# A fourth Strassen pair in four blocks of a fused attention and GEGLU kernel, with its helper sums and snapshots moved between engines

## The chip, the cores and the metric

The kernel runs on one core of a Trainium2 chip. The time is the device time of one execution in microseconds; for the kernel before it is the median of 8 runs. A profile records one execution instruction by instruction. Its engines are PE (TensorE, matrix multiply, with its weight loads listed apart as PEld), DVE (VectorE), ACT (ScalarE), POOL (GpSimd) and SP (SyncE, which issues DMAs here). Each engine works through its own instruction queue in order and waits on semaphores for the others.

## The reference

The computation is a linear attention followed by a gated feed-forward block. Inputs are q, k, v of 8 batches x 8 heads x 576 positions x 64, and three weight matrices of a width of 512 and a hidden width of 1536.

```python
q_s = np.exp(q - q.max(-1, keepdims=True)); q_s /= q_s.sum(-1, keepdims=True)
k_s = np.exp(k - k.max(2, keepdims=True));  k_s /= k_s.sum(2, keepdims=True)
kv = np.einsum('bhsd,bhse->bhde', k_s, v)
attn = np.einsum('bhsd,bhde->bhse', q_s, kv)
x = attn.transpose(0, 2, 1, 3).reshape(4608, 512)
g = x @ w_gate
out = (gelu(g) * (x @ w_val)) @ w_out
```

## The kernel before

**Blocks.** The 4608 rows are worked through in nine blocks: 0 to 7 hold 512 rows of each batch, and block 8 holds the 64 rows that each batch has over. The order is 0 to 6, then 8, then 7 (`order`, line 530). All matrices are in fp16 with sums in PSUM, which has eight banks; a small ring of bank names (`big`, `let_go`, lines 80 to 94) hands them out in turn.

**Hidden tiles.** For each block the hidden width is cut into 12 tiles of 128 (0 to 11). For each tile, g = x @ w_gate and v = x @ w_val are computed with the tile's rows as partitions, ScalarE takes Gelu of g and VectorE multiplies it with v into `ht`. Blocks 0 and 1 do this tile by tile (`ffn_fi`, line 475). From block 2 on a written-out list of steps sets the order of the work (lines 610 to 614): an entry such as `6g` or `6v` is one half of a tile done plainly (`half`, line 617: four matmuls of 512 columns), an entry such as `0.1` to `0.4` is one quarter of a pair (`pair_step`, line 627), and a single word such as `a`, `n` or `s0` is a place where other work rides along (`ride`, line 976, with the plan of lines 945 to 973).

**Pairs.** A pair k stands for the two tiles k and k + 3 and is computed as one 2 x 2 block product by Strassen's method in Winograd's form: seven products instead of eight, each of four matmuls of 256 columns (`product_gv`, line 594). Its quarters are: .1, products 1 and 5; .2, products 6 and 3; .3, products 7 and 2; .4, product 4. They run in three banks (pga, pgb, pgc). Between the products other engines work on the banks: ScalarE copies pga to pgb (line 660) and takes two snapshots `snq` (line 640; the one of product 5 is on VectorE in blocks 8 and 7, line 638), VectorE adds a snapshot to a bank into `cc` (line 644; the buffer alternates with one that lies in `eq`), and `final` finishes a lower quarter of a tile: Gelu on ScalarE (line 630), multiplication into `ht` on VectorE, here called the gate (line 631). `upper` finishes both upper quarters of the pair: Gelu in place on ScalarE (line 648), multiplication on GpSimd, or for pair 8 on VectorE (line 650). For pair 8 `upper` is put off until after the next entry of the list (lines 677 and 688).

A product writes to a bank only when the copy or add that reads it has finished: product 6 waits for the copy, product 7 for the second snapshot, product 3 for the first, product 4 for the add out of pga.

The list `THREE` (blocks 2 to 6) has the pairs 0, 1, 2 and the other six tiles in halves; `SIX` (blocks 8 and 7) has all six pairs 0, 1, 2, 6, 7, 8. Pairs need sums of weight blocks (`sum_wgv`, line 579) and of x (`sum_x`, line 588, on GpSimd). The weight sums for the pairs 6 to 8 are made on VectorE, three tiles at a time, one or two sums in each of the blocks 2 to 6 (line 972). Sum 3 writes over the weights that it reads.

**Output product.** `out_strassen` (line 722) multiplies `ht` by w_out in the same seven-product form with banks psa, psb, psc (`product`, line 702); the order is 1, 2, 5, 6, 3, 7, 4, and from block 2 on the tiles come in the order 0, 3, 1, 4, 2, 5 within a product. It needs sums of `ht` (`sum_h`, line 565): sums 1 and 2 on VectorE, 3 and 4 on GpSimd; the list has them at `s0`, `u0`, `s1`, `u1`, and the last two tiles' sums follow inside `out_strassen` (`last_js`). Snapshots `sn` (line 738) and adds into `yo` (line 748) are on VectorE, and the finished rows are stored by DMA.

**Riding work.** In each of the blocks 2 to 6 the attention of the next batches rides along. At `a` and `n`, `norm_pair` (line 235) sums exp(q) over the head width on VectorE and multiplies by the reciprocal on GpSimd; at `t`, `unit_td` transposes the result by a DMA; at `l`, the batch after next is loaded; at `e`, inside product 1 of the output, ScalarE takes the exponentials of q and k; at NS 0 the k-v product is made, and at NS 4 the next x (`unit_x4`, line 421), whose copies are split between ScalarE and VectorE. `cast_v` converts v on GpSimd at NS 2. `norm_rem0` and `unit_trem` do the same for the 64 rows that batch 0 has over.

Of the kernel before, what the change touches and what calls it, by code (L numbers as in the profile page):

```python
# [18 lines left out]
def kernel(  # L19
# [215 lines left out]
    def norm_pair(b, g, n0, engs):  # L235

        n = NC - n0
        e = buf(eq_b, b)[:, n0:NC, 2 * g * P:(2 * g + 2) * P].rearrange("p n (h d) -> p n h d", d=D)
        rq = att.tile([P, n, 4], f32, name="rq2", tag="rq2", bufs=2)
        nc.vector.reduce_sum(rq, e, axis=mybir.AxisListType.X)  # L240
        rrq = att.tile([P, n, 4], f32, name="rrq2", tag="rrq2", bufs=2)
        nc.vector.reciprocal(out=rrq, in_=rq)  # L242
        for j, eng in enumerate(engs):
            st[(b, "norm", 2 * g + j)] = (e[:, :, 2 * j:2 * j + 2], rrq[:, :, 2 * j:2 * j + 2], n)
            norm_mul(b, 2 * g + j, eng)
# [30 lines left out]
    st = {}  # L276
# [301 lines left out]

    def sum_wgv(nm, i, k=0, n=NO // 2):
        w = wg_sb if nm == "g" else wv_sb  # L580
        lo, hi = slice(k * P, (k + n) * P), slice((k + NO // 2) * P, (k + NO // 2 + n) * P)
        a11, a21, a12, a22 = w[:, 0:2, lo], w[:, 0:2, hi], w[:, 2:4, lo], w[:, 2:4, hi]
        t = [ws[(nm, k // NO)][:, j, :, k % NO * P:(k % NO + n) * P] for j in range(3)]
        o, a, b, op = {1: (t[0], a21, a22, ALU.add), 2: (t[1], t[0], a11, ALU.subtract),
                       3: (a21, a11, a21, ALU.subtract), 4: (t[2], a12, t[1], ALU.subtract)}[i]
        nc.vector.tensor_tensor(out=o, in0=a, in1=b, op=op)

# [6 lines left out]
    def product_gv(i, ps, xt, k, first):  # L594
# [3 lines left out]
        for t, w, nm in ((0, wv_sb, "v"), (1, wg_sb, "g")):  # L598
            ss = ws[(nm, k // NO)]
            for c in range(2):  # L600
# [8 lines left out]

    THREE = ("a 6g l 6v 0.1 9g 0.2 9v 0.3 7g 0.4 n 1.1 t 7v 1.2 10g 1.3 s0 10v 1.4 2.1 u0 8g 2.2 s1"  # L610
             " 8v 2.3 u1 11g 2.4 11v")
    SIX = ("0.1 6.1 0.2 6.2 0.3 6.3 0.4 1.1 6.4 7.1 s0 1.2 7.2 1.3 u0 7.3 1.4 2.1 7.4 8.1 s1 2.2"
           " 8.2 2.3 u1 8.3 2.4")
    steps = {b: (SIX if b >= B - 1 else THREE).split() for b in range(2, B + 1)}
    live = {}
# [11 lines left out]
    def pair_step(b, xt, k, i):  # L627
# [38 lines left out]
        if i == 2:  # L666
            product_gv(6, pa, xt, k, False)
            s2 = snap(pa)
            product_gv(3, pc, xt, k, False)
            add(cc[:, 0], pc, s2)  # L670
            let_go(pc)
        elif i == 3:
            product_gv(7, pa, xt, k, False)
            add(cc[:, 1], pa, s5)
            product_gv(2, pb, xt, k, False)
            final(pb, k)
            if k == NFI - NO // 2 - 1:
                live["upper"] = lambda: upper(cc)
            else:
                upper(cc)  # L680
        else:
            product_gv(4, pa, xt, k, False)
            final(pa, k + NO // 2)

    def go_on(b, xt, upto=None):
        while steps[b] and upto != 0:
            x = steps[b].pop(0)
            late = live.pop("upper", None)
            if "." in x:
# [32 lines left out]
    def out_strassen(b, last):  # L722
# [14 lines left out]

        def snap(nm):
            sn = ffn.tile([P, 2, 256], f32, name="sn", tag="gl")
            for n, (t, src) in enumerate(parts(nm)):  # L740
                if n:
                    nc.scalar.activation(out=sn[:, t], in_=src, func=ACTF.Copy, scale=1.0 / _H_SCALE)
                else:
                    nc.vector.tensor_scalar(out=sn[:, t], in0=src, scalar1=1.0 / _H_SCALE,
                                            scalar2=None, op0=ALU.mult)
            return sn
# [8 lines left out]
        get("a")  # L755
        product(1, ps["a"], True, js=js[:4])
        ride(b, NS, 0)
        if b >= B - 1:
            pair_step(b, get_x(b), NFI - NO // 2 - 1, 4)
        ride(b, PR, "e")  # L760
        get("b")
        product(1, ps["a"], False, js=js[4:])
        sum_h(*last_js(b), (1, 2))
        s1 = snap("a")
        product(2, ps["b"], True, js=js)
# [6 lines left out]
        sum_h(*last_js(b), (3,), "pool" if b > 1 else "dve")  # L772
        s5 = snap("c")
        ride(b, NS, 1)
        product(6, ps["a"], False, js=js)
        s2 = snap("a")
        ride(b, NS, 2)
# [167 lines left out]
    for b in range(2, B):  # L945
        n = b + 1
        if n < B:
            at(b, PR, "a", L(norm_pair, n, 0, 0, ("pool", "pool")))
            at(b, PR, "n", L(norm_pair, n, 1, 0, ("pool", "pool")))
            at(b, PR, "t", L(unit_td, n))  # L950
# [5 lines left out]
    at(4, PR, "e", exp_rem0)  # L956
    at(6, PR, "t", L(unit_trem, 0))
    for b in range(2, B - 1):
# [5 lines left out]
        at(b, NS, 4, L(lambda n: sum_x(get_x(n)), n if n < B - 1 else B))  # L964
        if b == 5:
            at(b, NS, 4, norm_rem0)
    at(B, NS, 2, L(lambda: sum_x(get_x(B - 1), xs_b[1])))
    for b in range(2, B + 1):
        for j in range(NO // 2 - 1):
            at(b, PR, f"s{j}", L(sum_h, j, NO, (1,)), L(sum_h, j, NO, (3,), "pool"))  # L970
            at(b, PR, f"u{j}", L(sum_h, j, NO, (2,)), L(sum_h, j, NO, (4,), "pool"))
    for b, x in ((2, "g1"), (2, "g2"), (3, "v1"), (3, "v2"), (4, "g4"), (5, "v4"), (6, "g3"), (6, "v3")):
        at(b, NS, 2, L(sum_wgv, x[0], int(x[1]), NO, NO // 2))

# [67 lines left out]
```

## Time and profile before

| | |
|---|---|
| median of 8 runs | 296.94 us (296.82 to 297.18) |
| the profiled execution | 296.96 us |
| its span, first to last instruction | 295.2 us |
| granted TensorE clock | 1.000 |
| matmuls | 2401 |
| block 2, 80.7 to 113.1 us: busy PE / DVE / ACT / POOL | 32.22 / 24.82 / 22.85 / 24.11 us |
| block 5, 174.0 to 204.4 us: the same | 30.40 / 21.74 / 20.98 / 23.29 us |

Times in the profile's rows are microseconds from the span's start. A timeline row gives the start, the duration, the engine, the source line, the operation, what it writes and reads, shapes, and how many equal instructions in a row were merged; in brackets stands the idle time of that engine before it and who ended it. Matmuls are pipelined: a single row's duration is longer than the distance to the next start, and the distance between starts is what counts. A row of the groups gives the count, the busy time, the mean duration of one in nanoseconds, and the idle time before them.

### The profile page before, as it was taken

What the parts mean: (1) busy time and instruction counts of PE and PEld (TensorE: products, weight loads), DVE (VectorE), ACT (ScalarE), POOL (GpSimd) and SP (SyncE); (2) the same over time, 40 slices, a digit from 0 to 9 for tenths busy, and PEclk for the clock granted to TensorE, in tenths of its full rate; (3) what the DMA queues carried; (4) which work ended last, traced back from release to release, by engine and by line L of the source; (5) the groups of instructions that cost most, each with busy time, mean ns of one, the idle gap of its engine ahead of it and who ended that gap; (6) DMA issues with size and microseconds to landing.
All of it is one profiled execution on the core that took longest, in us unless ns stands there. A gap on an engine that the chain in (4) does not pass through costs nothing. (4 is left out here: it accounts for less than half of the span.)

```text
span 295.2 us, 6183 instructions
## 1 busy us (share of the span) xinstructions
PE 285.1 (97%) x2401; PEld 198.5 (67%) x2401; DVE 219.9 (74%) x411; ACT 182.0 (62%) x295; POOL 196.2 (66%) x179
## 2 busy tenths in 40 slices
PE   3999999999999999999999999999999999999994
PEld 1444445446767686668666866687667888888884
DVE  2855888878978687867777676767677788958892
ACT  3763367776777658667756966695652477327640
POOL 1568647870496877687768776967886366673770
PEclk9999999999999999999999999999999999999999
DMA  6999999998069505970499029901140110033003
GB/s 219 373 382 389 401 390 392 341 321 229 3 231 383 100 3 175 383 155 3 142 352 237 2 106 343 265 2 73 71 91 10 73 72 2 1 72 72 2 0 144
DMA packets 54621, 51.72 MB, mean 175 GB/s; under 512 B 18496, under 2 KB 50496, under 8 KB 54592
## 3 DMA queue, kind: packets, MB, share of 16 engines
q1 hardware_dynamic: 52864, 49.49, 52.7%
q10 hardware_dynamic: 1728, 1.84, 1.9%
q8 instruction: 19, 0.31, 0.4%
q14 instruction: 10, 0.08, 0.1%
HBM read 37.75 MB, written 9.44 MB: 160 GB/s over the span
## 5 line engine op out<-in xcount | busy, mean ns | idle before, releaser
L466 PE MATMUL psg<-xt,wg_sb 128*128 128x512 f16 x216 | 57.5, 379 | 0.0
L466 PE MATMUL psv<-xt,wv_sb 128*128 128x512 f16 x216 | 57.4, 379 | 0.0
L249 POOL TENSOR_TENSOR eq<-eq,rrq 128x640 f16<-128x640 f16 (+1 forms) x27 | 34.7, 1302 | 20.1 <-DVE rrq L242 16.2
L712 PEld LDWEIGHTS <-ht 128*128 128x128 f16 x384 | 36.8, 98 | 8.6 <-issue 2.7
L466 PEld LDWEIGHTS <-wv_sb 128*128 128x128 f16 x216 | 21.0, 98 | 20.1 <-issue 0.5
L466 PEld LDWEIGHTS <-wg_sb 128*128 128x128 f16 x216 | 21.1, 98 | 18.6
L575 POOL TENSOR_TENSOR s<-ht,sh 128x512 f16<-128x512 f16 x21 | 25.3, 1206 | 9.4 <-DVE sh L575 9.4
L575 POOL TENSOR_TENSOR ht<-ht 128x512 f16<-128x512 f16 x21 | 25.2, 1199 | 5.5 <-DVE sh L575 5.5
L188 POOL CAST v<-vt 128x640 f16<-128x640 f32 x26 | 20.0, 813 | 12.9 <-PE pskv L342 11.3
L605 PEld LDWEIGHTS <-wv_sb 128*128 128x128 f16 x216 | 20.9, 98 | 11.2 <-issue 1.8
L650 POOL TENSOR_TENSOR ht<-eq 128x512 f16<-128x512 f32 x12 | 15.4, 1284 | 16.2 <-ACT eq L648 16.0
L471 ACT ACTIVATE gl<-psg 128x512 f32<-128x512 f32 x24 | 13.8, 598 | 16.9 <-PE psg L466 15.8
L712 PE MATMUL psa<-tw,ht 128*128 128x256 f16 x192 | 23.4, 272 | 0.4 <-DVE yo L750 0.4
L630 ACT ACTIVATE glq<-pgb 128x256 f32<-128x256 f32 x27 | 10.3, 380 | 21.9 <-PE pgb L605 14.0
L605 PEld LDWEIGHTS <-wg_sb 128*128 128x128 f16 x216 | 21.1, 98 | 2.5
L472 DVE SCALAR_TENSOR_TENSOR ht<-psv,gl 128x512 f16<-128x512 f32 x24 | 16.0, 686 | 8.7 <-PE psv L466 6.8
L212 ACT ACTIVATE ek<-kt 128x1280 f16<-128x1280 f32 (+1 forms) x11 | 19.1, 1748 | 5.2 <-DMA kt<-in_k_dram 3.7
L660 ACT COPY pgb<-pga 128x512 f32<-128x512 f32 x27 | 15.8, 584 | 9.8 <-PE pga L605 9.5
L622 ACT ACTIVATE gl<-psg 128x512 f32<-128x512 f32 x30 | 17.7, 590 | 5.7 <-PE psg L466 5.7
L240 DVE TENSOR_REDUCE rq<-eq 128x20 f32<-128x1280 f16 (+1 forms) x12 | 17.1, 1427 | 4.6 <-ACT eq L212 4.6
L712 PEld LDWEIGHTS <-sh 128*128 128x128 f16 x192 | 18.8, 98 | 2.4 <-issue 0.3
L212 ACT ACTIVATE eq<-qt 128x2560 f16<-128x2560 f32 (+2 forms) x10 | 18.4, 1863 | 2.6 <-DMA qt<-in_q_dram 2.5
(164 smaller groups left out, 679.9 us busy)
## 6 DMA issues: line engine op xcount, KB each, us to landing
out_dram<-yo SPq DMA_DIRECT2D x15, 512.0 KB, 3.5
kt<-in_k_dram SPq DMA_DIRECT2D x7, 640.0 KB, 9.1
vt<-in_v_dram SPq DMA_DIRECT2D x7, 640.0 KB, 5.1
qt<-in_q_dram SPq DMA_DIRECT2D x7, 640.0 KB, 7.6
qt<-in_q_dram SPq DMA_DIRECT2D x8, 512.0 KB, 8.1
wost<-in_moe_w_out_dram SPq DMA_DIRECT2D x6, 512.0 KB, 7.9
kt<-in_k_dram SPq DMA_DIRECT2D x6, 512.0 KB, 9.8
vt<-in_v_dram SPq DMA_DIRECT2D x6, 512.0 KB, 5.8
```

The source lines that it names most:

```text
L188: nc.gpsimd.tensor_copy(out=dst, in_=src)
L212: nc.scalar.activation(out=dst[:, n0:NC, h0 * D:h1 * D].rearrange(o, d=D, **({"t": 2} if b >= QUAD else {})), in_=heads(tiles[(nm, b)], b, ...
L240: nc.vector.reduce_sum(rq, e, axis=mybir.AxisListType.X)
L249: (nc.gpsimd if eng == "pool" else nc.vector).tensor_tensor(out=e, in0=e, in1=rrq.unsqueeze(-1).to_broadcast((P, n, 2, D)), op=ALU.mult)
L466: nc.tensor.matmul(ps, w[:, ci, fi * P:(fi + 1) * P], xt[:, ci, :], start=(ci == 0), stop=(ci == HP - 1))
L472: nc.vector.scalar_tensor_tensor(out=ht[:, fi, :], in0=psv, scalar=_H_SCALE, in1=gl, op0=ALU.mult, op1=ALU.mult)
L575: (nc.gpsimd if eng == "pool" else nc.vector).tensor_tensor(out=o, in0=a, in1=b, op=op)
L605: nc.tensor.matmul(ps[:, t], a, x, start=(first and t == 0 and c == 0), stop=(c == 1), skip_group_check=True)
L622: nc.scalar.activation(out=live[c], in_=t, func=ACTF.Gelu)
L650: (nc.vector if k == NFI - NO // 2 - 1 else nc.gpsimd).tensor_tensor(out=ht[:, k:k + NO // 2 + 1:NO // 2, 256:512], in0=cc[:, :, 0], in1=c ...
L660: nc.scalar.copy(out=pb, in_=pa)
L712: nc.tensor.matmul(ps[t], a, w, start=(first and j == js[0] and (t == ts[0] or ps[t].tensor is not ps[ts[0]].tensor)), stop=(j == js[-1]), ...
```

## The change

- Blocks 3 to 6 get a list `FOUR`: pair 6 (tiles 6 and 9) is added, interleaved with pair 0, and the halves 6g, 6v, 9g, 9v go. Quarter 2.4 is no longer in the list; it is issued inside output product 1, after the first three of its tiles, and the sum `u1` follows there.
- The weight sums for pair 6 are made on GpSimd in block 2, one tile at a time, four at `w` and four at `x`. Those of the pairs 7 and 8 stay on VectorE, two tiles at a time, two sums in each of the blocks 3 to 6.
- `norm_pair` at `n` makes only the sums and reciprocals; its two multiplications on GpSimd stand at a new place `m`. In `FOUR` `n` comes before the pairs and `m` after 6.3; in block 2 they stand together.
- From block 2 on, except block 7, the output's first snapshot is on ScalarE, straight after product 1, and the exponentials at `e` are issued after it. In block 8 the other two output snapshots are on ScalarE as well.
- In `SIX` `s1` moves from before 2.2 to after 2.3, and `u1` from after 2.3 to after 8.3.
- Where a quarter .4 is followed by a quarter .1 in the list, its `final` is put off until after that next quarter.
- The remainder's norm and transposition move to `r` in block 6.

```diff
-        for j, eng in enumerate(engs):
-            st[(b, "norm", 2 * g + j)] = (e[:, :, 2 * j:2 * j + 2], rrq[:, :, 2 * j:2 * j + 2], n)
+        for j in range(2):
+            st[(b, "norm", 2 * g + j)] = (e[:, :, 2 * j:2 * j + 2], rrq[:, :, 2 * j:2 * j + 2], n)
+        for j, eng in enumerate(engs):
             norm_mul(b, 2 * g + j, eng)
...
-    THREE = ("a 6g l 6v 0.1 9g 0.2 9v 0.3 7g 0.4 n 1.1 t 7v 1.2 10g 1.3 s0 10v 1.4 2.1 u0 8g 2.2 s1"
-             " 8v 2.3 u1 11g 2.4 11v")
-    SIX = ("0.1 6.1 0.2 6.2 0.3 6.3 0.4 1.1 6.4 7.1 s0 1.2 7.2 1.3 u0 7.3 1.4 2.1 7.4 8.1 s1 2.2"
-           " 8.2 2.3 u1 8.3 2.4")
-    steps = {b: (SIX if b >= B - 1 else THREE).split() for b in range(2, B + 1)}
+    THREE = ("a 6g l 6v 0.1 9g 0.2 9v w 0.3 7g 0.4 n m 1.1 t 7v 1.2 10g 1.3 s0 10v 1.4 2.1 u0 8g 2.2 s1"
+             " 8v 2.3 u1 11g 2.4 11v x")
+    FOUR = ("a 7g l 7v n 0.1 6.1 0.2 6.2 0.3 6.3 m 10g 0.4 6.4 1.1 t 10v 1.2 s0 8g u0 1.3 8v 1.4 r 2.1"
+            " 11g s1 2.2 11v 2.3")
+    SIX = ("0.1 6.1 0.2 6.2 0.3 6.3 0.4 1.1 6.4 7.1 s0 1.2 7.2 1.3 u0 7.3 1.4 2.1 7.4 8.1 2.2"
+           " 8.2 2.3 s1 8.3 u1 2.4")
+    steps = {b: (SIX if b >= B - 1 else THREE if b == 2 else FOUR).split() for b in range(2, B + 1)}
...
             if k == NFI - NO // 2 - 1:
-                live["upper"] = lambda: upper(cc)
+                live["late"] = lambda: upper(cc)
             else:
                 upper(cc)
         else:
             product_gv(4, pa, xt, k, False)
-            final(pa, k + NO // 2)
+            if steps[b] and steps[b][0].endswith(".1"):
+                live["late"] = lambda: final(pa, k + NO // 2)
+            else:
+                final(pa, k + NO // 2)
...
-            late = live.pop("upper", None)
+            late = live.pop("late", None)
...
-        def snap(nm):
+        def snap(nm, act=False):
...
-                if n:
+                if n or act:
...
         get("a")
-        product(1, ps["a"], True, js=js[:4])
+        four = 2 < b < B - 1
+        cut = 3 if four else 4
+        product(1, ps["a"], True, js=js[:cut])
+        if four:
+            pair_step(b, get_x(b), NO // 2 - 1, 4)
+            product(1, ps["a"], False, js=js[cut:4])
         ride(b, NS, 0)
+        if four:
+            ride(b, PR, "u1")
         if b >= B - 1:
             pair_step(b, get_x(b), NFI - NO // 2 - 1, 4)
-        ride(b, PR, "e")
         get("b")
         product(1, ps["a"], False, js=js[4:])
+        if b > 1 and not last:
+            s1 = snap("a", True)
+        ride(b, PR, "e")
         sum_h(*last_js(b), (1, 2))
-        s1 = snap("a")
+        if b < 2 or last:
+            s1 = snap("a")
...
-        s5 = snap("c")
+        s5 = snap("c", b == B)
...
-        s2 = snap("a")
+        s2 = snap("a", b == B)
...
-            at(b, PR, "n", L(norm_pair, n, 1, 0, ("pool", "pool")))
+            at(b, PR, "n", L(norm_pair, n, 1, 0, ()))
+            at(b, PR, "m", L(norm_mul, n, 2, "pool"), L(norm_mul, n, 3, "pool"))
...
-    at(6, PR, "t", L(unit_trem, 0))
+    at(6, PR, "r", norm_rem0, L(unit_trem, 0))
...
-        if b == 5:
-            at(b, NS, 4, norm_rem0)
...
-    for b, x in ((2, "g1"), (2, "g2"), (3, "v1"), (3, "v2"), (4, "g4"), (5, "v4"), (6, "g3"), (6, "v3")):
-        at(b, NS, 2, L(sum_wgv, x[0], int(x[1]), NO, NO // 2))
+    for i, xs_ in (("w", ("g1", "v1", "g2", "v2")), ("x", ("g4", "v4", "g3", "v3"))):
+        for x in xs_:
+            at(2, PR, i, L(sum_wgv, x[0], int(x[1]), NO, 1, "pool"))
+    for b, x in ((3, "g1"), (3, "g2"), (4, "v1"), (4, "v2"), (5, "g4"), (5, "v4"), (6, "g3"), (6, "v3")):
+        at(b, NS, 2, L(sum_wgv, x[0], int(x[1]), NO + 1, 2))
```

## The prediction

> **What bounds the kernel now.** I read the page's busy times first, then the matmul cadence in TensorE's timeline, then every place where that cadence breaks, and last the queues of VectorE, ScalarE and GpSimd at those places.
>
> ```profile
> PE 285.1 (97%) x2401; PEld 198.5 (67%) x2401; DVE 219.9 (74%) x411; ACT 182.0 (62%) x295; POOL 196.2 (66%) x179
> ```
>
> TensorE sets the time: 97% busy, nobody else above 74%. A busy PE in this record says little about its pace, so I take the pace from starts. From TensorE's timeline in block 1:
>
> ```profile
> 61.37 1.03 PE L466 MATMUL psv<-xt,wv_sb 128*128 128x512 f16 x4
> ...
> 70.01 1.03 PE L466 MATMUL psv<-xt,wv_sb 128*128 128x512 f16 x4
> 70.87 1.47 PE L712 MATMUL psa<-wo_sb,ht 128*128 128x256 f16 x12
> 72.18 1.47 PE L712 MATMUL psb<-wo_sb,ht 128*128 128x256 f16 x12
> ```
>
> Forty matmuls of 512 columns start between 61.37 and 70.01: 8.64 / 40 = 0.216 us each. Twelve of 256 columns take 72.18 - 70.87 = 1.31: 0.109 each; those of the pairs keep the same pace (four in 0.44 on the chain of waits). From block 2 on nearly every matmul starts at this pace, so time is won by fewer columns or by closing a gap in the pace. The gaps: each block's 11g is followed by its last quarter 0.11 us late (blocks 3 to 6; 0.17 in block 2), because product 4 waits for VectorE's add out of the same bank. Block 2's last output product waits 0.32 us where blocks 3 to 5 wait 0.10. Blocks 8 and 7 each lose 0.11 + 0.13 + 0.06 + 0.25 = 0.55 us around steps 2.2 to 2.4, and block 8 0.27 + 0.07 more where output products wait for snapshots on VectorE. The largest of these in block 8, all engines in order of time:
>
> ```profile
> 251.99 0.68 DVE L644 SCALAR_TENSOR_TENSOR eq<-pga,snq 128x512 f32<-128x512 f32 x1
> ...
> 252.25 0.38 PE L605 MATMUL pgb<-xtr,wg_sb 128*128 128x256 f16 x2
> ...
> 252.72 0.38 PE L605 MATMUL pga<-xs,wv_sb 128*128 128x256 f16 x2
> ```
>
> The add ends at 252.67 and product 4 starts at 252.72 instead of 252.47.
>
> **The change, part by part.** The sum is made against the profiled execution: 296.96 us with a span of 295.2, which is the median of the runs shown (296.94) within 0.02, so the 1.8 us around the span is kept and differences carry over.
>
> *The fourth pair, blocks 3 to 6.* Out go 6g, 6v, 9g, 9v: 16 matmuls x 0.216 = 3.46 us. In come 28 x 0.109 = 3.06. That is -0.40 a block, -1.6 in all, all of it on TensorE's path. The Trainium skill speaks against this step: "TensorE: Matmul & The Clock Gate", section "Back-to-back issue gap", gives about 131 ns for a 512-column matmul in a sustained stream and 81 ns for 128 columns; an estimate by that page, 98 ns for 256 columns on the straight line between, would make the pair 28 x 98 - 16 x 131 = 0.65 us slower a block. The starts above decide against it.
>
> Whether TensorE is fed: ScalarE gains a copy (0.58), two snapshots (0.60 each), two Gelus of 256 (0.38 each) and one of 0.63 for two Gelus of 0.59, so +2.0 us a block; its stretch of a block is 21 busy of 30.4. VectorE gains 2 x 0.68 + 2 x 0.42 - 2 x 0.67 = +0.9 (22 of 30.4), GpSimd one multiply, +1.28 (23 of 30.4). All fit on average. The tight place is the start: pairs 0 and 6 run with no half between. I lay ScalarE's queue against TensorE in block 5's frame (0.1 starts at 175.30, each step 0.875). ScalarE starts operations queued behind each other 0.51 apart (248.94 and 249.45). Copy of pair 0 at 176.00, its snapshot 176.48, copy of pair 6 177.0, its snapshot 177.5, second snapshots 178.0 and 178.5. Product 7 of pair 0 is due at 178.80 and needs the one ending at 178.6: 0.14 us to spare. No wait, cost 0; if that cover goes, each 0.1 us costs 0.1 in each of four blocks.
>
> *The last quarter (2.4) inside output product 1.* It now comes 1.53 us after product 7 started (1.74 before), with one gate (0.60) ahead of the add on VectorE in place of a gate and a sum (0.60 + 0.33). Product 7's result is there after 0.6, the add may start at 0.79 and end at 1.47: just in time. Bounds: the old 0.11 wait wholly gone (-0.46 in all) or kept (0). I take -0.25. The finished tile 5 needs Gelu 0.38 and gate 0.42 behind 2.4 and is used after eight columns' worth of matmuls and kv (0.75 us), 0.25 us to spare.
>
> *Snapshot 1 on ScalarE, exponentials behind it.* The exponentials started 2.1 us before product 1 ended; now they start a snapshot (0.6) after it, 2.85 us later. What hides that, in block 4, the fullest:
>
> ```profile
> 169.01 0.40 ACT L263 ACTIVATE eq0r<-eq 64x256 f16<-64x256 f32 x1
> 171.91 0.27 ACT L190 CAST xtr<-psxr 128x128 f16<-128x128 f32 x1 [2.49 <-PE psxr L429]
> ...
> 176.00 0.57 ACT L660 COPY pgb<-pga 128x512 f32<-128x512 f32 x1 [0.31 <-PE pga L605]
> ```
>
> 2.49 us of idle time take 2.85 with 0.36 left over, and the 0.31 before 176.00 takes most of the rest; blocks without the remainder's two exponentials (0.7) have 0.3 to spare. I take +0.1 in all; 0 to +0.6.
>
> *Weight sums on GpSimd in block 2.* Eight sums of 256 elements. The nearest rows give the price of one:
>
> ```profile
> L592 POOL TENSOR_TENSOR xs<-xt 128x512 f16<-128x512 f16 x10 | 11.5, 1154 | 8.5 <-ACT xt L190 8.5
> L556 POOL TENSOR_TENSOR tw<-wo_sb,tw 128x1536 f16<-128x1536 f16 x1 | 3.1, 3092 | 0.0
> ```
>
> (3.09 - 1.15) / 1024 = 1.9 ns an element, so 0.67 us each, 2.7 for each group of four. The second group ("x") delays the last sums, idle 1.51 us before them, by 1.2; product 7, which needs the last, starts at 108.9 and the sum is ready at 108.5: hidden, and if the sums cost a 512-element row (1.15) the wait is 1.5 us. In exchange VectorE's two sums of 1.11 and 0.95 leave the place just ahead of the add that block 2 waits for: 0.32 becomes 0.10, -0.2. Bounds -0.2 to +1.3; I take -0.2, the scaled price being nearest. Splitting the norm (sums early, multiplies at "m") leaves the transposing DMA where it was: GpSimd frees it near 186.3, against 186.5. The remainder's norm and transposition move to "r" in block 6, ahead of the stores on SP and still some 7 us before their use. The smaller VectorE sums in blocks 3 to 6 cost and win nothing: gaps there are 0.10 with one sum or two.
>
> *Blocks 8 and 7.* Taking the second sums out from 2.2 and sending the Gelus of finished quarters behind the next step's copies lets the copies and snapshots that TensorE waited for start 0.3 to 0.7 us sooner: the 0.55 us can go, and in block 8 also the 0.27 + 0.07, by snapshots on ScalarE. But "8.3 u1 2.4" also reverses an order. Before, the deferred upper half of pair 8 came behind 2.4; now u1 draws it ahead. So on VectorE the order after pair 8's add becomes gate, sum, multiply of the upper half, and only then the gate of quarter 2.4, which makes tile 5, the last weights of product 1. How it stood:
>
> ```profile
> 253.25 0.68 DVE L644 SCALAR_TENSOR_TENSOR cc<-pga,snq 128x512 f32<-128x512 f32 x1
> ...
> 254.02 0.63 ACT L648 ACTIVATE cc<-cc 128x512 f32<-128x512 f32 x1
> 254.03 0.38 PE L605 MATMUL pga<-xs,wv_sb 128*128 128x256 f16 x2
> ...
> 254.18 0.41 DVE L631 SCALAR_TENSOR_TENSOR ht<-pga,glq 128x256 f16<-128x256 f32 x1
> ...
> 254.69 0.69 DVE L650 TENSOR_TENSOR ht<-cc 128x512 f16<-128x512 f32 x1
> ```
>
> The add ends at 253.93; the gate that ends at 254.59 was in time for tile 5's turn at 254.68. Now, from the add's end: Gelu 0.06 + 0.63, multiply from 0.75, the gate 0.60 after the multiply's start, ending at 1.76. TensorE is at tile 5 at 0.10 + 0.44 + 0.22 = 0.76. It waits 1.0 us, in both blocks, against 0.55 saved: +0.45 in block 7, +0.45 - 0.34 = +0.1 in block 8, together +0.55. A VectorE sum that met GpSimd at work took 1.04 instead of 0.42, so I add 0.15: +0.7. Bounds: -1.45 (all waits gone) to +1.8 (both chains slowed by 0.6).
>
> **Sum:** -1.6 - 0.25 + 0.1 - 0.2 + 0.7 = -1.25, so 295.7.
>
> **Rivals.** *The reorder works (0.15).* If TensorE comes to tile 5 late enough, or the gate is not behind the multiply, blocks 8 and 7 give -1.3: -1.6 - 0.35 - 0.2 - 1.3 = -3.45, 293.5. For it: 0.55 us of plain waits; against it: the order just counted.
> *Nothing to tell (0.15).* The waits at tile 5 grow to 1.5 us each (+1.6) and the 0.11 gaps stay: -1.6 - 0.2 + 0.1 + 1.3 = -0.4, 296.5. For it, the 1.04 sum.
> *ScalarE becomes the bound at the block starts (0.17): slower.* The late exponentials push table load, copy and the first Gelu into the six queued operations. Cover is 0.3 + 0.31 + 0.14 = 0.75 us; what goes past it, TensorE pays in each of four blocks at product 7 of pair 0. From 0.46 us past it a block the -1.25 turns to +0.6; one more wait of a table load's length (1.28) gives 0.55 a block, +2.2, 297.9. For it: the idle time left is the smallest of all; against it: the table loads keep their number.
>
> **How the numbers follow.** The forecast has 0.53, its own range 295.0 to 296.3. Leaving out the slower rival and the edge of the fastest, the range is 293.4 to 296.9. About 0.2% (0.59 us) is what a measurement of this kernel can tell from no change. Faster by more than that: 0.51 + 0.15 = 0.66; within: 0.02 + 0.15 = 0.17; slower: 0.17.
>
> **What would show it.** 2449 matmuls; blocks 3 to 6 of 29.9 to 30.1 us instead of 30.4; the last quarter starting with no gap; no gap above 0.1 us before product 7 of pair 0. In blocks 8 and 7 one gap of about 1 us before the last two matmuls of product 1, ended by VectorE's L631 gate behind the L650 multiply, and the four old gaps gone. The forecast is wrong if that gap is missing (then nearer 293.5), or if product 7 waits for ScalarE's snapshot, or product 7 of block 2 for GpSimd.

## The result and the profile after

| | before | after |
|---|---|---|
| median | 296.95 us (296.77 to 297.27, 31 runs) | 300.70 us (298.89 to 302.46, 11 runs) |
| ratio to before | | 1.012 (95% interval 1.0102 to 1.0138) |
| profiled execution, its span | 296.96, 295.2 us | 300.86, 299.1 us |
| granted TensorE clock of it | 1.000 | 0.994 |
| matmuls | 2401 | 2449 |

The changed kernel is slower. Its executions lie at three levels: four at 298.9 to 299.2 us with a granted clock of 1.000, four at 300.5 to 300.9 with 0.994, three at 302.2 to 302.5 with 0.988 or 0.989. (A twelfth execution on record, at 302.50 us with 0.989, is not in the median.) The profile is from the middle level. One execution of the kernel before, among nine taken beside experiment 12, took 301.36 us with a clock of 0.993; it is left out of that ratio, and no profile tells its cause.

From the page of the changed kernel, the busy times and the row of the granted clock in 40 slices of the span:

```profile
PE 285.3 (95%) x2449; PEld 204.2 (68%) x2449; DVE 226.3 (76%) x411; ACT 194.1 (65%) x319; POOL 206.3 (69%) x191
...
PEclk9999999999999999999999999999999999799999
```

TensorE is busy about as long as before and its share fell, so the span grew by time in which it waited. One slice of the clock row, the 35th (254 to 262 us), is no longer at full speed.

Measured from the start of the first matmul of a block's hidden tiles to the same of the next block (for block 7, to the start of the last matmul), the blocks changed like this (us):

| block | 2 | 3 | 4 | 5 | 6 | 8 | 7 |
|---|---|---|---|---|---|---|---|
| before | 30.67 | 30.43 | 30.43 | 30.43 | 30.64 | 27.16 | 29.35 |
| after | 30.62 | 30.01 | 30.06 | 30.07 | 30.67 | 30.29 | 31.15 |
| difference | -0.04 | -0.42 | -0.37 | -0.36 | +0.03 | +3.13 | +1.80 |

Blocks 2 to 6 gave 1.16 us, blocks 8 and 7 took 4.93; with 0.12 us ahead of block 2 that is the 3.9 us by which the spans differ.

The wait in block 8, all engines in order of time, in the changed kernel (TensorE's last matmuls of product 1 are at the end):

```profile
251.70 0.68 DVE L647 SCALAR_TENSOR_TENSOR cc<-pga,snq 128x512 f32<-128x512 f32 x1
...
251.92 1.27 POOL L653 TENSOR_TENSOR ht<-eq 128x512 f16<-128x512 f32 x1 [2.56 <-ACT eq L651]
...
252.63 0.84 DVE L576 TENSOR_TENSOR sh<-sh,ht 128x512 f16<-128x512 f16 x1
...
252.91 0.38 PE L718 MATMUL psa<-wo_sb,ht 128*128 128x256 f16 x2
...
253.15 1.33 POOL L576 TENSOR_TENSOR ht<-ht 128x512 f16<-128x512 f16 x1
253.40 1.63 DVE L653 TENSOR_TENSOR ht<-cc 128x512 f16<-128x512 f32 x1
...
254.95 0.74 DVE L634 SCALAR_TENSOR_TENSOR ht<-pga,glq 128x256 f16<-128x256 f32 x2
...
255.42 0.39 PE L718 MATMUL psa<-wo_sb,ht 128*128 128x256 f16 x2 [2.13 <-DVE ht L634]
```

Read it from the bottom. Tile 5's matmuls wait for the gate (L634), the gate stands behind the upper half's multiply (L653) on VectorE, and that behind u1's sum (L576). The multiply takes 1.63 us; before the change it took 0.69. The sum takes 0.84 instead of 0.41. The two matmuls before the wait start at 252.91 and 253.02, the next at 255.42: 2.40 us where the pace is 0.11, so 2.29 are lost. (The 2.13 in brackets counts from the modelled end of the matmul before.) Block 7 has the same rows with the same lengths and the same 2.29.

What comes after the wait, as busy time by stretch of 2 us (columns: the stretch, its length, then busy time and count of PE, PEld, DVE, ACT and POOL, then the granted clock, the DMA share and GB/s):

```profile
252.00:254.00 2.00, 1.29 (x12) 0.91 (x10) 2.00 (x4) 1.29 (x4) 2.00 (x2) 1.00 0.00 0
254.00:256.00 2.00, 0.58 (x6) 0.53 (x7) 2.00 (x4) 0.09 (x1) 2.00 (x2) 0.99 0.00 0
256.00:258.00 2.00, 2.00 (x12) 1.45 (x10) 0.75 (x2) 0.51 (x1) 1.18 (x3) 0.50 0.03 8
258.00:260.00 2.00, 2.00 (x14) 1.51 (x13) 0.69 (x1) 0.00 (x0) 2.00 (x3) 0.65 0.00 0
260.00:262.00 2.00, 2.00 (x20) 1.80 (x19) 0.00 (x0) 1.15 (x2) 1.92 (x3) 1.00 0.00 0
```

The clock is halved from 256 to past 259. Sixteen matmuls of 256 columns start 0.213 us apart instead of 0.109: 16 x 0.104 = 1.7 us lost, with no engine in the way. In block 7 of this execution the clock stayed up. The difference of 3.13 - 1.80 = 1.33 between the two blocks is this 1.7 less the 0.34 of snapshot waits that only block 8 had to lose. The three levels of the times are 1.7 us apart too: no, one or two such stretches.

The predicted small gaps did close. The 0.25 us wait ahead of product 4 in pair 2 is under 0.05, and those of 0.11, 0.13 and 0.06 are gone in both blocks, as are the 0.27 and 0.07 in block 8. Block 6 has a new one. From TensorE's timeline there, with its last quarter in the second row:

```profile
221.77 0.82 PE L718 MATMUL psa<-wo_sb,ht 128*128 128x256 f16 x6
222.83 0.38 PE L606 MATMUL pga<-xs,wv_sb 128*128 128x256 f16 x2 [0.23 <-DVE cc L647]
```

The last of the six starts at 222.32 and the next matmul 0.51 us later: 0.40 us lost waiting for the add into `cc`, which blocks 3 to 5 don't lose.

### The profile page after: what moved, and what is told of

It is laid out like the page before. It is cut to its first block, busy times and chain, and to the rows that moved or that the text cites. A ratio compares the mean times of both kernels' runs of the same rounds, so it can differ in the third digit from the quotient of the medians.

```text
span 299.1 us, 6345 instructions
## 1 busy us (share of the span) xinstructions
PE 285.3 (95%) x2449; PEld 204.2 (68%) x2449; DVE 226.3 (76%) x411; ACT 194.1 (65%) x319; POOL 206.3 (69%) x191
## 4 chain that ended last, share of the span: by engine, by line
PE 83%; DVE 9%; ACT 2%; DMA 2%; POOL 1%; issue 1%; ACTq 0%; DVEq 0%
PE pga L606 15%; PE psa L718 13%; PE psv L467 12%; PE psg L467 12%; PE pgc L606 8%; PE psc L718 7%; PE psb L718 4%; PE pgb L606 4%; PE psy L535 3%; DMA qt<-in_q_dram 2%; PE pskv L343 2%; DVE cc L647 1%; DVE sh L576 1%; DVE ht L653 1%; ACT snq L643 1%
## 5 line engine op out<-in xcount | busy, mean ns | idle before, releaser
L467 PE MATMUL psg<-xt,wg_sb 128*128 128x512 f16 x184 | 49.3, 379 | 0.0
L467 PE MATMUL psv<-xt,wv_sb 128*128 128x512 f16 x184 | 49.2, 379 | 0.0
L653 POOL TENSOR_TENSOR ht<-eq 128x512 f16<-128x512 f32 x14 | 17.8, 1271 | 21.3 <-ACT eq L651 21.3
L576 POOL TENSOR_TENSOR s<-ht,sh 128x512 f16<-128x512 f16 x21 | 25.6, 1219 | 6.1 <-DVE sh L576 6.1
L576 POOL TENSOR_TENSOR ht<-ht 128x512 f16<-128x512 f16 x21 | 25.6, 1219 | 5.9 <-DVE sh L576 5.9
L634 DVE SCALAR_TENSOR_TENSOR ht<-pga,glq 128x256 f16<-128x256 f32 x31 | 12.9, 421 | 16.0 <-ACT glq L633 15.8
L472 ACT ACTIVATE gl<-psg 128x512 f32<-128x512 f32 x24 | 13.8, 598 | 16.6 <-PE psg L467 16.5
L653 POOL TENSOR_TENSOR ht<-cc 128x512 f16<-128x512 f32 x15 | 19.1, 1275 | 7.5 <-ACT cc L651 7.5
L633 ACT ACTIVATE glq<-pgb 128x256 f32<-128x256 f32 x31 | 11.7, 379 | 18.7 <-PE pgb L606 10.9
L663 ACT COPY pgb<-pga 128x512 f32<-128x512 f32 x31 | 18.0, 580 | 5.1 <-PE pga L606 4.8
L643 ACT ACTIVATE snq<-pga 128x512 f32<-128x512 f32 x31 | 18.5, 598 | 4.0 <-PE pga L606 3.7
```

The costliest lines, as they stand in the source:

```text
L467: nc.tensor.matmul(ps, w[:, ci, fi * P:(fi + 1) * P], xt[:, ci, :], start=(ci == 0), stop=(ci == HP - 1))
L472: nc.scalar.activation(out=gl, in_=psg, func=ACTF.Gelu)
L576: (nc.gpsimd if eng == "pool" else nc.vector).tensor_tensor(out=o, in0=a, in1=b, op=op)
L643: nc.scalar.activation(out=sn, in_=ps, func=ACTF.Copy, scale=_H_SCALE)
L653: (nc.vector if k == NFI - NO // 2 - 1 else nc.gpsimd).tensor_tensor(out=ht[:, k:k + NO // 2 + 1:NO // 2, 256:512], in0=cc[:, :, 0], in1=c ...
L663: nc.scalar.copy(out=pb, in_=pa)
```

## The experiments

Unless said otherwise, each kernel is the changed kernel with the edit shown. All were compared with the kernel before on the same chip. The experiments ran on four chips, on which the kernel before had medians of 296.96 to 297.00 us, so their times can be compared with each other.

**1. u1 behind the gate of tile 5.**

```diff
-           " 8.2 2.3 s1 8.3 u1 2.4")
+           " 8.2 2.3 s1 8.3 2.4 u1")
```

> In SIX, u1 stands behind 2.4 again, so the gate of quarter 2.4 is ahead of the multiply of pair 8's upper half. Theory (the queue order on VectorE makes the wait before tile 5): both waits of 2.29 us shrink to under 0.2, no execution shows a lowered clock, and the time is that of the executions with an undisturbed clock less 2 x 2.2: 299.0 - 4.4 = 294.6, with a scatter under 0.5 us. Rival (the moved sum s1, the deferred gates or ScalarE's output snapshots make the wait): the waits keep over 1 us each and the time stays above 297.

Measured: 297.08 us (296.97 to 297.38, 11 runs), ratio 1.0004 (0.9996 to 1.0013). The wait at tile 5 is gone, which shows the order to be its cause. But 294.6 was missed by 2.5 us. In the timeline of block 8, all engines:

```profile
252.88 0.69 DVE L653 TENSOR_TENSOR ht<-cc 128x512 f16<-128x512 f32 x1
252.89 1.69 POOL L576 TENSOR_TENSOR ht<-ht 128x512 f16<-128x512 f16 x1
...
253.49 1.37 DVE L576 TENSOR_TENSOR sh<-sh,ht 128x512 f16<-128x512 f16 x1
254.78 0.41 DVE L634 SCALAR_TENSOR_TENSOR ht<-pga,glq 128x256 f16<-128x256 f32 x1
...
255.25 0.39 PE L718 MATMUL psb<-wo_sb,ht 128*128 128x256 f16 x2 [0.91 <-DVE ht L634]
```

The wait moved to the next gate, that of tile 11 (quarter 8.4), the last weights of product 2: it stands behind u1's sum, which now takes 1.37 us. That is 1.07 us lost in each of the two blocks, and in block 7 another 0.34 ahead of product 6.

**2. The wait filled with matmuls.** Eight matmuls of 512 columns between tile 2 and tile 5 of product 1 in blocks 8 and 7; nothing uses their results.

```diff
+        if b >= B - 1:
+            product(1, ps["a"], False, js=js[4:5])
+            fill = big([P, 512], f32, "fill")
+            for _ in range(8):
+                nc.tensor.matmul(fill, ident, warm, start=True, stop=True)
+            product(1, ps["a"], False, js=js[5:])
```

> In blocks 8 and 7, eight matmuls of 512 columns with a constant operand (1.7 us of work into a bank that nobody reads) stand in the wait before tile 5; they add work that the result does not use. Theory (the lowered clock follows TensorE's idle time): the filled wait leaves about 0.5 us idle, the clock is 1.00 in all executions, and all lie at 299.0 to 299.3, without the steps to 300.7 and 302.3. Rival (the clock falls for another reason, such as the load of the denser blocks before): the three steps stay.

Measured: 299.11 us (298.87 to 299.32, 5 runs), granted clock 0.999 to 1.000 in all five. TensorE's timeline in block 8:

```profile
253.27 1.89 PE L778 MATMUL fill<-warm,ident 128*128 128x512 f16 x8
255.56 0.39 PE L718 MATMUL psa<-wo_sb,ht 128*128 128x256 f16 x2 [0.41 <-DVE ht L634]
255.79 1.25 PE L718 MATMUL psb<-wo_sb,ht 128*128 128x256 f16 x10
```

Tile 5 starts as late as before, 2.29 us behind its turn, of which the filling leaves 0.57 idle, but the ten matmuls behind it come at full pace and the upper two levels are gone. The lowered clock is a consequence of the idle time, and the wait alone makes 299.1.

**3. GpSimd kept quiet.** The sums 3 and 4 of s1 and u1 in blocks 8 and 7 are made on VectorE, behind both gates; the order of the rest stays.

```diff
+        ride(b, PR, "p")
         sum_h(*last_js(b), (1, 2))
...
-            at(b, PR, f"s{j}", L(sum_h, j, NO, (1,)), L(sum_h, j, NO, (3,), "pool"))
-            at(b, PR, f"u{j}", L(sum_h, j, NO, (2,)), L(sum_h, j, NO, (4,), "pool"))
+            behind = b >= B - 1 and j == 1
+            at(b, PR, f"s{j}", L(sum_h, j, NO, (1,)))
+            at(b, PR, f"u{j}", L(sum_h, j, NO, (2,)))
+            at(b, PR, "p" if behind else f"s{j}", L(sum_h, j, NO, (3,), "dve" if behind else "pool"))
+            at(b, PR, "p" if behind else f"u{j}", L(sum_h, j, NO, (4,), "dve" if behind else "pool"))
```

> In blocks 8 and 7 the third and fourth sums of s1 and u1 are on VectorE behind both gates instead of on GpSimd, so GpSimd is idle during the multiply of pair 8's upper half. Theory (the multiply takes 1.63 us instead of 0.69 because GpSimd is in a sum at the same time): it takes 0.7, the wait falls from 2.29 to 1.35 us, and executions with an undisturbed clock take 299.0 - 1.9 = 297.1; whether 1.35 us of idle time still lowers the clock is open. Rival (the multiply is slow for its operands or place): it keeps 1.6 and the wait 2.2 us.

Measured: 297.17 us (296.99 to 297.44, 11 runs), ratio 1.0006 (0.9997 to 1.0015). VectorE and TensorE in block 8:

```profile
252.52 0.84 DVE L576 TENSOR_TENSOR sh<-sh,ht 128x512 f16<-128x512 f16 x1
...
253.29 0.68 DVE L653 TENSOR_TENSOR ht<-cc 128x512 f16<-128x512 f32 x1
253.89 0.74 DVE L634 SCALAR_TENSOR_TENSOR ht<-pga,glq 128x256 f16<-128x256 f32 x2
254.36 0.39 PE L718 MATMUL psa<-wo_sb,ht 128*128 128x256 f16 x2 [1.17 <-DVE ht L634]
```

With the same queue and no sum on GpSimd beside it, the multiply takes 0.68 us and the loss at tile 5 is 1.34 in both blocks, so 0.95 of the 2.29 was GpSimd's sums. The 0.84 stays, since GpSimd's multiply of the other upper half is still there.

**4. Blocks 8 and 7 as before the change.** Their list, their gates and their output snapshots; blocks 2 to 6 stay changed.

```diff
-    SIX = ("0.1 6.1 0.2 6.2 0.3 6.3 0.4 1.1 6.4 7.1 s0 1.2 7.2 1.3 u0 7.3 1.4 2.1 7.4 8.1 2.2"
-           " 8.2 2.3 s1 8.3 u1 2.4")
+    SIX = ("0.1 6.1 0.2 6.2 0.3 6.3 0.4 1.1 6.4 7.1 s0 1.2 7.2 1.3 u0 7.3 1.4 2.1 7.4 8.1 s1 2.2"
+           " 8.2 2.3 u1 8.3 2.4")
...
-            if steps[b] and steps[b][0].endswith(".1"):
+            if b < B - 1 and steps[b] and steps[b][0].endswith(".1"):
...
-        if b > 1 and not last:
+        if 1 < b < B - 1:
...
-        if b < 2 or last:
+        if b < 2 or b >= B - 1:
...
-        s5 = snap("c", b == B)
+        s5 = snap("c")
...
-        s2 = snap("a", b == B)
+        s2 = snap("a")
```

> Blocks 8 and 7 are as before the change (list, gates, snapshots); blocks 2 to 6 as changed. By the two traces blocks 2 to 6 are 1.16 us shorter, so the theory (the whole loss sits in blocks 8 and 7) gives 296.95 - 1.1 = 295.8, without scatter. Rival (the fourth pair disturbs the blocks behind it): 297 or more.

Measured: 295.93 us (295.65 to 296.06, 5 runs), ratio 0.9962 (0.9949 to 0.9974). The work on blocks 2 to 6 gains 1.0 us by itself, as its block lengths say. All of the loss is in blocks 8 and 7.

**5. Both gates first.** Quarter 2.4 follows 8.3 at once, as in experiment 1, and u1 is issued only after quarter 8.4 and its gate.

```diff
-           " 8.2 2.3 s1 8.3 u1 2.4")
+           " 8.2 2.3 s1 8.3 2.4")
...
             pair_step(b, get_x(b), NFI - NO // 2 - 1, 4)
+            ride(b, PR, "u1")
```

> The changed kernel with the two gates ahead of everything else on VectorE: the list of blocks 8 and 7 ends 2.3 s1 8.3 2.4, and u1 is issued behind quarter 8.4 (tile 11). Theory (both waits, 2.29 us at tile 5 in the changed kernel and 1.07 us at tile 11 when u1 stood behind 2.4, are a gate queued behind a VectorE instruction of two operands in memory that GpSimd slows): neither wait is left, because the gate of tile 11 loses the 1.37 us sum ahead of it and had waited 1.07 us. From the 297.08 us of the run with u1 behind 2.4, less 2 x 1.07 and less the matmuls of about 0.4 us at the lowered clock: 294.5 us, and no matmul at a lowered clock. Rival (the order is not the cause, GpSimd's speed is: the multiply itself, ahead of the gate of tile 11, now takes 1.6 us against GpSimd's sum of s1): a wait of 0.3 to 0.6 us at tile 11, 295.2 to 295.8 us.

Measured: 295.76 us (295.62 to 295.90, 5 runs), ratio 0.9960 (0.9946 to 0.9973). Neither gate is waited for in either block: the theory holds for both, and the rival's wait at tile 11 isn't there. The time still missed the expected 294.5, because a third wait appeared, in block 7 only. All engines there:

```profile
282.75 1.27 POOL L576 TENSOR_TENSOR s<-ht,sh 128x512 f16<-128x512 f16 x1 [0.36 <-DVE sh L576]
283.04 1.26 DVE L576 TENSOR_TENSOR sh<-sh,ht 128x512 f16<-128x512 f16 x1
...
284.21 0.41 DVE L750 TENSOR_SCALAR sn<-psa 128x256 f32<-128x256 f32 x1
...
284.68 0.49 PE L718 MATMUL psa<-tw,sh 128*128 128x256 f16 x3 [1.00 <-DVE sn L750]
```

In the last block half of product 1's snapshot is on VectorE, behind the sums. It is late by what the sums have grown, and product 6, which writes to the same bank, loses 1.17 us.

**6. The remainder's norm back in block 5.** On top of 5.

```diff
-    at(6, PR, "r", norm_rem0, L(unit_trem, 0))
+    at(6, PR, "t", L(unit_trem, 0))
...
+        if b == 5:
+            at(b, NS, 4, norm_rem0)
```

> The kernel with the gates first, and the normalization of the rest (norm_rem0) issued at the end of block 5 and its transposes at t of block 6, as before the change, in place of both at r of block 6. Theory (the 0.40 us wait ahead of the last quarter in block 6 comes from VectorE and GpSimd being late by the normalization at r): the wait goes, 0.40 us less than the kernel with the gates first, 294.1 us. Rival (the wait stands where two units end and moves to another tile or to block 5): the same time within 0.15 us.

Measured: 297.06 us (296.94 to 297.29, 11 runs), 1.3 us more than experiment 5. Both theories fell. The 0.40 us wait of block 6 went, as the first says, but a larger one came at the start of block 6, at pair 6, which the new list puts at the very start. The row of TensorE's timeline:

```profile
206.47 0.38 PE L606 MATMUL pgc<-xs,wsv 128*128 128x256 f16 x2 [1.36 <-POOL xs L593]
```

GpSimd's multiply of the remainder (1.04 us, with a wait of 2.45 for VectorE ahead of it) now stands before `sum_x`, and the pair, for want of `xs`, loses 1.53 us by its pace. Ahead of unit 1's last quarter in the same block the wait grew too, from 0.16 to 0.41 us. The old place is too dear with the new list, and "r" is the cheaper of the two; that the pair at the start of the list is what makes the difference is read from this row, and no run puts it elsewhere.

**7. The gates at once.** On top of 5, in blocks 8 and 7 the gate of a last quarter is no longer put off.

```diff
-            if steps[b] and steps[b][0].endswith(".1"):
+            if b < B - 1 and steps[b] and steps[b][0].endswith(".1"):
```

> The kernel with the gates first, but in blocks 8 and 7 the gate of a unit's last quarter is issued at once, as before the change, not behind the next unit's first step. Theory (the deferred gates remove the waits of 0.115, 0.134 and 0.057 us at the second unit's steps): these come back, 2 x 0.31 us, 295.1 us. Rival (the moved sums removed them): the same time as the kernel with the gates first, within 0.1 us.

Measured: 296.15 us (296.07 to 296.30, 8 runs), 0.39 more than experiment 5. The gaps of 0.12, 0.13 and 0.06 are back at the same three matmuls in both blocks, so it is the deferred gates that removed them: between the profiled executions the spans differ by 0.5 us. (The expected 295.1 was counted from the 294.5 expected of experiment 5.)

**8. The last block's snapshot first.** On top of 5: product 1's snapshot in block 7 on ScalarE, ahead of u1 and the sums; in both blocks u1 moves behind this snapshot.

```diff
-            ride(b, PR, "u1")
...
-        if b > 1 and not last:
+        if b > 1:
             s1 = snap("a", True)
+        if b >= B - 1:
+            ride(b, PR, "u1")
         ride(b, PR, "e")
         sum_h(*last_js(b), (1, 2))
-        if b < 2 or last:
+        if b < 2:
             s1 = snap("a")
```

> The kernel with the gates first, and in the last block (7) the snapshot of product 1 on ScalarE ahead of the sums, as in block 8, in place of one half on each engine behind them. Theory (the 1.17 us wait ahead of product 6 in block 7 of the kernel with the gates first is this snapshot, queued on VectorE behind u1's and the last tiles' sums, which took 1.04 and 1.26 us beside GpSimd): it goes, 295.76 less 1.17: 294.6 us, no wait over 0.3 us from block 8 to the end. Rival (the sums in front of product 5 or 6 are late themselves, or ScalarE's snapshot of product 5 is): a wait of 0.4 us or more at another place of block 7, 295.0 us or more.

Measured: 294.99 us (294.92 to 295.11, 5 runs), ratio 0.9933 (0.9921 to 0.9946). The 1.17 us wait is gone; a new one of 0.52 stands ahead of product 3, which waits for the half of product 5's snapshot that is still behind the sums on VectorE. That is the rival's number within 0.01 us, and the snapshot that it names, but the half on VectorE and not one on ScalarE.

**9. The remainder's norm split.** On top of 8: sums behind product 5 of block 5, multiply on VectorE at "r".

```diff
-        nc.gpsimd.tensor_tensor(
+        st["rem0"] = e, rrq
+
+    def mul_rem0():
+        e, rrq = st["rem0"]
+        nc.vector.tensor_tensor(
...
-    at(6, PR, "r", norm_rem0, L(unit_trem, 0))
+    at(5, NS, 1, norm_rem0)
+    at(6, PR, "r", mul_rem0, L(unit_trem, 0))
```

> The kernel with the snapshot first, and the normalization of the rest in two parts: its sum and reciprocal behind product 5 of block 5, its multiply at r of block 6 on VectorE and not on GpSimd. Theory (the 0.40 us wait ahead of the last quarter in block 6 is VectorE made late at r by 0.87 us of sum and reciprocal and by a sum of h that takes 1.25 us and not 0.42 beside GpSimd's multiply): it goes but for 0.1 us, 0.3 us less than the kernel with the snapshot first. Rival (VectorE has no 0.9 us to spare behind product 5 of block 5): the wait comes back there, the same time or more.

Measured: 294.62 us (294.54 to 294.99, 5 runs), 0.37 less than experiment 8, and the 0.40 us wait of block 6 is gone. The theory holds; which of the two parts of the edit does it is open.

**10. A longer wait, once.** On top of 8: six copies of 128x512 on VectorE ahead of tile 5's gate in block 8.

```diff
+        def idle(ps):
+            d = ffn.tile([P, 2, 256], f32, name="snq", tag="snq")
+            for _ in range(6):
+                nc.vector.tensor_scalar(out=d, in0=ps, scalar1=1.0, scalar2=None, op0=ALU.mult)
...
+            if b == B and k == 2:
+                idle(pa)
```

> The kernel with the snapshot first and, in block 8 alone, six copies of 128x512 on VectorE ahead of tile 5's gate (their results are not used), so that TensorE waits there once for some 3.5 to 4 us. Theory (a long enough idle time lowers TensorE's clock every time; at 2.29 us it did so in some executions, at 1.07 to 1.34 us in none): one step in all executions, 3.5 to 4 us of wait and about 1.7 us of slower matmuls, 299.8 to 300.4 us in one level within 0.5 us, granted clock about 0.994. Rival (it is chance, not length): two levels 1.7 us apart again.

Measured: 301.41, 301.52, 302.18 and 302.35 us, with granted clocks of 0.993, 0.994, 0.988 and 0.989. The wait was longer than meant, 4.79 us. The stretches of 2 us, columns as above:

```profile
256.00:258.00 2.00, 0.23 (x2) 0.23 (x3) 1.36 (x4) 1.13 (x3) 0.00 (x0) 0.97 0.00 0
258.00:260.00 2.00, 2.00 (x11) 1.38 (x10) 1.97 (x5) 0.64 (x2) 0.76 (x1) 0.50 0.03 8
260.00:262.00 2.00, 2.00 (x14) 1.55 (x13) 1.48 (x2) 0.00 (x0) 1.64 (x3) 0.67 0.00 0
262.00:264.00 2.00, 2.00 (x21) 1.79 (x19) 0.00 (x0) 0.81 (x2) 2.00 (x3) 1.00 0.00 0
```

The clock was lowered in every execution, as the theory says, and again for sixteen matmuls in the profiled one: 294.99 + 4.79 + 1.7 = 301.5, the lower two times. The two others lost 0.8 us more at a lower clock still, so there are two levels, which the theory had not, though not 1.7 apart, as the rival had it. One lowered stretch of 3.41 us takes 3.41 x 0.5 / 300 = 0.006 from the mean clock, so by this estimate 0.994 is one stretch and 0.988 two. Why a second one came is open; no profile fell on the upper level.

**11. u0 later.** On top of 8, in blocks 3 to 6.

```diff
-    FOUR = ("a 7g l 7v n 0.1 6.1 0.2 6.2 0.3 6.3 m 10g 0.4 6.4 1.1 t 10v 1.2 s0 8g u0 1.3 8v 1.4 r 2.1"
+    FOUR = ("a 7g l 7v n 0.1 6.1 0.2 6.2 0.3 6.3 m 10g 0.4 6.4 1.1 t 10v 1.2 s0 8g 1.3 8v u0 1.4 r 2.1"
```

> The kernel with the snapshot first, and in blocks 3 to 6 the sums u0 behind unit 1's third step and the half 8v, not ahead of it. Theory (the waits of 0.14 us ahead of unit 1's last quarter are VectorE's sums s0 and u0 ahead of its addition): they go, 4 x 0.14, 0.55 us less than the kernel with the snapshot first. Rival (the sum on GpSimd, now later, meets the multiply of unit 1 and makes a gate late): the same or up to 0.5 us more.

Measured: 294.43 us (294.25 to 294.59, 4 runs), 0.56 less than experiment 8, the predicted number. The waits ahead of unit 1's last quarter (0.09, 0.15, 0.15 and 0.15 us in blocks 3 to 6 of experiment 8) are gone, and so is the 0.40 of block 6; against them a 0.41 us wait appeared in block 8, ahead of quarter 2.4, and its cause is open. The match is partly luck: two effects that weren't foreseen cancel.

**12. Product 5's snapshot on ScalarE in the last block too.** On top of 11.

```diff
-        s5 = snap("c", b == B)
+        s5 = snap("c", b >= B - 1)
```

> The kernel with u0 later, and in the last block (7) the snapshot of product 5 on ScalarE alone, as in block 8. Theory (the wait of 0.52 us ahead of product 3 in block 7 of the two kernels before is the half of this snapshot that stands on VectorE behind the sums of 1.04 and 1.26 us and two additions): it goes but for 0.1 us, 294.43 less 0.4: 294.0 us. Rival (the snapshot of product 6, half on each engine, is then the late one, or ScalarE is): a wait of 0.3 us or more ahead of product 7, 294.3 to 294.5 us.

Measured: 294.26 us (294.14 to 294.52, 5 runs), ratio 0.9910 (0.9896 to 0.9924). The wait ahead of product 3 is gone, and 0.34 us comes back in product 7, behind its first two matmuls. That is the rival's wait in size and, nearly, in place, but not its cause: the snapshot of product 6 was done by 284.80, and the third matmul, at 286.08, waits for GpSimd's sum 3 of the last tiles (284.88 + 1.15 = 286.03). From the timeline of block 7:

```profile
284.42 0.38 ACT L748 ACTIVATE sn<-psa 128x256 f32<-128x256 f32 x1 [0.76 <-PE psa L718]
...
284.88 1.15 POOL L576 TENSOR_TENSOR ht<-ht 128x512 f16<-128x512 f16 x1
...
286.08 1.16 PE L718 MATMUL psa<-tw,ht 128*128 128x256 f16 x9 [0.18 <-POOL ht L576]
```

The median is the lowest here, 2.7 us below the kernel before and 6.4 below the changed one; the runs of experiments 11 and 12 overlap (294.25 to 294.59 and 294.14 to 294.52).

## Why the prediction was wrong

The forecast was 295.7 us and faster; the median is 300.7 and slower. It erred by 5.0 us, at one place mostly.

- **Tile 5's wait: right place, right cause, wrong size.** "It waits 1.0 us, in both blocks" was the term. The gate did stand behind the multiply, TensorE came to tile 5 0.75 us after the add's end, and the wait ended by that gate. But the gate ended 2.98 us after the add's end (251.70 + 0.68 to 254.95 + 0.41), not 1.76. The step that failed is the allowance "so I add 0.15", for "A VectorE sum that met GpSimd at work": it took one such row for an occasional surcharge. Instead u1's sum took 0.84 for 0.42, so that the multiply began 0.27 later, and the multiply took 1.63 for 0.69; together these are the 1.22 us between 1.76 and 2.98. Of the 2.29 us, experiment 3 shows 0.95 to be GpSimd's sums beside the multiply; the rest, 1.34, is the order with the 0.84 sum. The term "+0.7" measured +3.2 at full clock (3.13 + 1.80 less the 1.7 of the lowered clock). Even the bound "+1.8 (both chains slowed by 0.6)" was too low, since each was slowed by 1.2.
- **The lowered clock was no term at all.** It adds 1.7 us for each wait after which it comes, 1.7 in the median execution. Experiment 2 shows that it goes with the idle time. Without it the changed kernel is at 299.1, still slower.
- **The fourth pair: right.** "-0.40 a block" stands against -0.42, -0.37 and -0.36 in blocks 3 to 5. All terms of blocks 2 to 6 together were -1.95, and experiment 4 shows 1.0 us of gain; the next three points hold the rest.
- **"I take -0.25" for the last quarter: moved, not won.** Its own gap is 0.01 as predicted. But 0.08 to 0.15 us came in its place ahead of unit 1's last quarter, behind the sums that the new list puts on VectorE just there (experiment 11 removes it).
- **The remainder at "r": costed at nothing.** The prediction looked at its due time and SP's queue and not at what is behind it on VectorE. It costs 0.40 us in block 6 (experiment 9).
- **Block 2: -0.04 for -0.2.** The 0.32 us wait became 0.10 as predicted, and the wait ahead of the last quarter grew from 0.17 to 0.34.
- **ScalarE: no cost, and the slower rival fell.** No gap stands ahead of product 7 of pair 0 in any block. (The "0.14 us to spare" is 0.20 by the two times beside it, 178.80 and 178.6; nothing hangs on it.) The slower outcome had 0.17, for a mechanism that didn't occur. The rival that was nearest, waits "grow to 1.5 us each", had the right mechanism and stopped short.

Could the size have been read before? In large part, and it is the lesson of the case. In the kernel before, VectorE and GpSimd in block 8 behind the rows that the prediction showed:

```profile
254.69 0.69 DVE L650 TENSOR_TENSOR ht<-cc 128x512 f16<-128x512 f32 x1
254.70 1.69 POOL L575 TENSOR_TENSOR s<-ht,sh 128x512 f16<-128x512 f16 x1
255.29 0.42 DVE L631 SCALAR_TENSOR_TENSOR ht<-pga,glq 128x256 f16<-128x256 f32 x1
255.63 1.04 DVE L575 TENSOR_TENSOR sh<-ht 128x512 f16<-128x512 f16 x1
```

The multiply that came first kept its 0.69, the GpSimd sum behind it was stretched, the gate in between was not, and the next sum took 1.04. Such rows, put side by side, say when a VectorE instruction with both operands in SBUF ends if it starts while GpSimd is at work on SBUF:

| kernel | VectorE's instruction | GpSimd's ends | VectorE's ends | after it |
|---|---|---|---|---|
| before, block 8 | sum, 255.63, 1.04 us | 256.39 | 256.67 | 0.28 |
| after, block 8 | sum, 252.63, 0.84 us | 253.19 | 253.47 | 0.28 |
| after, block 8 | multiply, 253.40, 1.63 us | 254.48 | 255.03 | 0.55 |
| experiment 1, block 8 | sum, 253.49, 1.37 us | 254.58 | 254.86 | 0.28 |
| experiment 5, block 7 | sum, 283.04, 1.26 us | 284.02 | 284.30 | 0.28 |

The end doesn't depend on the start: the instruction waits GpSimd's out and then needs 0.28 us (0.41 alone) or 0.55 (0.69 alone). The trace of the kernel before has twelve such sums of VectorE, which end 0.28 to 0.30 us after GpSimd's instruction. With GpSimd's multiply ending at 253.19 and its sum of 1.16 straight behind it, the rule puts the end of VectorE's multiply at 254.9; it was 255.03.

## What to carry to other kernels

Where a VectorE instruction with both operands in SBUF is moved ahead of something urgent, look at what GpSimd does when it starts and count its end as GpSimd's end and a little, not its own length. Taking an instruction out of one queue position moves the wait to the next consumer (tile 5, tile 11, product 6, product 3, product 7 here), so follow the queue to the end of the block before a gain is booked. And price a TensorE wait of some 2 us or more above its length, since its clock may be halved after it.

## What the runs showed of the hardware

*VectorE and GpSimd exclude each other on operands in SBUF.* In the traces of the changed kernel and of experiments 1, 3, 4, 5, 8 and 12, all 122 sums of VectorE that start while a GpSimd instruction of two operands runs, and more than 0.05 us before its end, end 0.277 to 0.349 us after it (median 0.281), whether they took 0.41 or 1.37. (Five more start in its last 0.02 us and take their 0.41.) It goes both ways: a GpSimd sum that finds VectorE at one takes up to 1.70 us instead of 1.16, as the second row of experiment 1 shows. Gates, which have one operand in PSUM, take 0.424 us in the middle of GpSimd's work and 0.415 outside it. The Trainium skill, "GPSIMD Engine Reference", section "8. Key points", says that GpSimd shares its SBUF interfaces with VectorE and contends with its instructions of two SBUF inputs. The rows agree, and in them the second to come waits for the whole of the first.

*The clock falls after less idle time than 3 us.* Lost pace of 1.07 us at a place (experiment 1) and of 1.34 us (experiment 3) brought no step of 1.7 us in 22 executions; 2.29 us brought it at about half of the places (levels of none, one or two in 4, 4 and 3 executions, two places each); 4.79 us in 4 of 4. The Trainium skill, "TensorE: Matmul & The Clock Gate", section "Why this matters for your kernels", asks for no idle gaps over some 3 us between bursts of matmuls. The 2.29 us here are under that and were enough. Its section "What's actually happening" gives a free-running window of about 3.4 us, and the lowered stretch agrees: sixteen matmuls of 0.213 are 3.4 us, in the changed kernel and in experiment 10.

The traces show what decides. In each of the 14, the granted clock changes only at times that lie whole multiples of 3.413 us apart; in the changed kernel these are 10.22, 255.97, 259.39 and 300.35 us, 72, 1 and 12 such windows apart. Cut at these times, the changed kernel's two waits look like this (columns as above; block 8's wait and the window behind it, then block 7's):

```profile
252.56:255.97 3.41, 1.28 (x12) 0.91 (x11) 3.41 (x6) 1.15 (x4) 3.41 (x3) 1.00 0.00 0
255.97:259.38 3.41, 3.41 (x18) 2.42 (x16) 1.47 (x3) 0.54 (x1) 2.59 (x4) 0.50 0.02 5
283.28:286.70 3.42, 1.61 (x15) 1.19 (x13) 3.42 (x6) 1.60 (x5) 3.19 (x3) 1.00 0.00 0
286.70:290.11 3.41, 3.10 (x29) 2.79 (x30) 2.89 (x8) 0.43 (x2) 2.59 (x3) 1.00 0.02 5
```

Block 8's wait of 2.29 us lies within one window, and the next runs at half the clock. Block 7's equal wait falls on a boundary, with 1.97 us in one window and 0.32 in the next, and the clock stays. Counted by pace over all 14 traces from the first rise of the clock on, each window with 2.30 us or more of idle time was followed by a lowered one (the end of the kernel included), and none with 1.97 or less. So a wait of this length costs 1.7 us more or nothing by where it falls, which is the chance in the levels; where between 1.97 and 2.30 us the limit lies, no run shows.
